# A Fourier filter and a mixer on one core: the prologue's roundings and loads in another order

## The chip, the cores and the metric

The kernel runs on one core of a Trainium2 chip. The metric is the device time of one execution in microseconds; where several are given, the median stands. The engines are TensorE (PE, the matrix unit; its weight loads are shown as PEld), VectorE (DVE), ScalarE (ACT), GpSimd (POOL) and SyncE (SP, which only issues transfers). Each engine executes its own instructions in program order. Transfers (DMA) are issued by SP, ACT and POOL and move data between DRAM and the on-chip memory.

## The reference

Two blocks run one after the other, on 8 batches of 3008 x 256 values. The first filters each column along its 3008 rows in the frequency domain. The second mixes along the rows (token weights, 3008 to 256 to 3008) and then along the columns (channel weights, 256 to 1536 to 256). The sizes below are those of the call.

```python
def _attn_ref(x, filt_r, filt_i):
    X = np.fft.rfft(x, axis=1)
    F = (filt_r + 1j * filt_i)[None, :, :]
    y = np.fft.irfft(X * F, n=x.shape[1], axis=1)
    return y.astype(np.float32)

def _moe_ref(x, w_tok1, w_tok2, w_ch1, w_ch2):
    xt = x.transpose(0, 2, 1)
    h = np.maximum(xt @ w_tok1, 0.0) @ w_tok2
    u = x + h.transpose(0, 2, 1)
    h2 = np.maximum(u @ w_ch1, 0.0) @ w_ch2
    return (u + h2).astype(np.float32)

# x: (8, 3008, 256), filt_*: (1505, 256), float32
# w_tok1: (3008, 256), w_tok2: (256, 3008), w_ch1: (256, 1536), w_ch2: (1536, 256), float64
```

The four weights come in as 8-byte floats and the kernel works in 4-byte floats, so it rounds them on the chip.

## The kernel before, in words

**The filter.** 3008 is 64 times 47. `dft` does a length-64 transform of a batch as 12 matmul steps (`a_unit`, the matmul at L454, one 128 x 512 tile each), and then 32 length-47 steps with the filter's products and the inverse (`b_unit`, matmul L514 and product L522 or L527 to L530; `bi_unit`, matmul L539). Batches go in groups: batch 0 alone, then (1, 2), (3, 4), (5, 6) and 7. `dft` is a generator; each `next` on it emits one step, so that its caller places the steps beside other work. For batch 0 the length-64 results stay on the chip. For the later ones, a step's result is copied by ACT (L460) and stored to `z_tmp`, from where it comes back turned. The inputs `x` of these steps have two buffers: the load for step u + 2 is issued on SP when step u has been emitted. The results of the inverse length-47 steps are stored to `g_tmp` by ACT's queue (L550), two steps to a store, and are read back turned, as six tiles `t4`, by SP (`t4_load`, L587). A row of `t4` is ready when the step that belongs to it has been stored: row r belongs to step r // 4.

**The mixer.** For each batch, `token_sums` (48 matmuls at L593) multiplies the first token weights `w1` with `t4`, ACT takes the maximum with zero (L605), and `u_unit` (for batch 0) multiplies with the second token weights `w2` and adds the filter's last transform (L615, L623). Then 36 *items* follow per batch, six column blocks `m` of six *channel pairs* `jp`. An item runs `up_first` (4 products, L716), the sums `up_middle`, a first part of the preceding pair's `down` (L750), `up_last` (3 products, L732), and the second part of `down`. The weights of the channel mixing are in `chan`, seven combinations to a pair, of which POOL makes some by sums (`combine`, L354 to L358). `mix` is also a generator: it yields after each part of an item (its *place*: 0, 1 or 2), and the main loop decides at each place whether the filter's generator of the next group takes one step there. While the length-64 steps of the first later group last, each place takes one; after that 35 steps are spread over 48 of the places 1 and 2.

**The rounding of the weights.** The weights are cut into 40 tiles, in this order: 12 of `w1`, 16 of `w2` (8 of 64 row groups each, 377 values wide, the last of each half 376), 2 of `w_ch1`, and the ten tiles named `LAST`. A tile passes four phases, each of which is one `next` on the tile's generator: *begin* (the loads; SP issues those of `w1`, POOL all the others), *copy* (one ACT copy of the high words, L260), *middle* (two DVE instructions, L262 and L263) and *end* (two DVE instructions, L266 and L268, and then the two halves are added). For the tiles of `w1` and the first four of `w2` the adding is done by two matmuls in PE (`on_chip`, L301 and L302, into one of the four banks `po`), which `sum_up` emits later, with an ACT copy behind them. For the other tiles DVE adds (L290). `convert_middle` does one middle phase and `sum_up`; `convert_end` does one end phase, one copy phase (two tiles ahead of the end phase), and lets `fill` begin further tiles, up to five beyond those ended (four for `LAST`). `convert` is both. A tile's loads go into a staging buffer that an earlier tile has to leave first. POOL makes the sums of `combine` at the end of a tile that completes a pair.

**The order around the change.** The whole program is emitted in one order by hand (`manual_schedule`). It is: the length-64 steps of batch 0; its length-47 steps `k`, with 20 of the 40 tiles spread beside them in half phases (`IN_B`), and within them the loads of rows 0 to 63 of `t4` (at k = 19 to 24) and of rows 64 to 111 (at k = 30 and 31); the loads of rows 112 to 127; `token_sums` of batch 0; the remaining eight `w1` and `w2` tiles; two more tiles around `u_unit`; then the items, of which the first five carry two tiles of `LAST` each, one ahead of `up_first` and one ahead of `up_last`.

Of the kernel before, what the change touches and what calls it, by code (L numbers as in the profile page):

```python
# [19 lines left out]
N1 = 47  # L20
N2 = 64
NF = N // 2 + 1
D = 256
P = 128
K2 = 32
A = 24
# [15 lines left out]
CW = 32  # L42
CB = P // CW
MT = 6
NG = 8
PARTS = (0, 64, 112)
BY_PE = 4
IN_B = 20
EARLY = 12
GROUPS = ((0,), (1, 2), (3, 4), (5, 6), (7,))  # L50

# [74 lines left out]
def kernel(  # L126
# [116 lines left out]

    early = [(up, "u")] * 2 + [(tp, "t")] * 2 + [(vp, "v")] * 2
    late = [(t2p, "t2"), (t3p, "t3")]
    stages = [(t4p, "t4")] * (A // 2) + early * 3 + late * 5

    def stage(n):
        where, tag = stages.pop(0)
# [76 lines left out]

    def w2_load(i):

        t, g = divmod(i, N2 // NG)
        n = NG * N1  # L330

        more = g + 1 < N2 // NG
        st = stage(512)
        nc.gpsimd.dma_start(st[:, 0:n + more], moe_w_tok2[ts(t, P), ds(g * n, n + more)])
        yield
        dst = w2[:, t].rearrange("p (a h n2) -> p h n2 a", h=2, n2=HALF)[:, :, ds(g * NG, NG), :]

        def some(h, nh, w):
            return (lambda v: bass.AP(tensor=v.tensor, offset=v.offset + h * A, ap=[v.ap[0], [A, nh], [N1, NG], [1, w]]),
                    dst[:, h:h + nh, :, 0:w])  # L340

        parts = [some(0, 2, A)] if more else [some(0, 1, A), some(1, 1, A - 1)]
        if i < BY_PE:
            h = halves(st, n + more, spare_pair())
            yield next(h)
            yield next(h)
            on_chip(ident, *next(h), n + more, parts)
        else:
            yield from rounded(st, n + more, parts, False)
# [23 lines left out]
    def wc2_load(i):  # L373
# [5 lines left out]
        def tile_of(dh):  # L379
# [7 lines left out]
    LAST = ((wc2_load, 0), (wc1_load, 1), (wc1_load, 4), (wc2_load, 1), (wc1_load, 2), (wc2_load, 2), (wc1_load, 5),  # L387
            (wc2_load, 3), (wc2_load, 4), (wc2_load, 5))

    tiles = ([w1_load(i) for i in range(A // 2)] + [w2_load(i) for i in range(TC * N2 // NG)]  # L390
             + [wc1_load(c * (DC // 512), False) for c in range(DH)] + [f(i) for f, i in LAST])
    begin, copy, middle, end = (iter(tiles) for _ in range(4))

    def advance(it):
        s = next(it, None)
        if s:
            next(s, None)
# [5 lines left out]
    def convert():  # L403

        convert_middle()
        convert_end()
# [5 lines left out]
    def convert_end():  # L412
        ended[0] += 1
        advance(end)
        advance(copy)
        fill(5)

    begun = [0]

    def fill(ahead):  # L420
        while begun[0] < len(tiles) and begun[0] < ended[0] + (4 if begun[0] >= len(tiles) - len(LAST) else ahead):
            start()
# [299 lines left out]
    def up_middle(hh, w, g, s):  # L722
        hw = w // 2
        u2 = hh[:, 2, 0:hw]
        v(u2, g[0][:, 1, 0:hw], s[:, 0])
        v(s[:, 1:3], g[1][:, :, 0:hw], u2.unsqueeze(1).to_broadcast([P, 2, hw]))
# [95 lines left out]
    def mix(next_ready):  # L822

        wait = []
        pos, hhs, tts = {}, {}, {}

        def loads(b):
            if b + 1 < B and next_ready(b):
                for c in wait:
                    t4_load(b + 1, c)  # L830
                wait.clear()


        own = ({(3, 2): 0, (4, 2): 1}, {(2, 2): 0, (3, 0): 1, (3, 2): 2, (4, 0): 3})
        new = {(JP - 3, 2): 0, (JP - 2, 0): 1, (JP - 2, 2): 2, (JP - 1, 0): 3}

        def u_parts(b, m, jp, place):
            parts = own[b > 0] if m + 1 < MT else new if b + 1 < B else {}
            part = parts.get((jp, place))
            if part is None:  # L840
                return
            b, m = (b, m + 1) if m + 1 < MT else (b + 1, 0)
            u_part(b, m, part)
            if part == len(parts) - 1:
                if m:
                    wait.append(m)
                todo_v.extend(v_steps(b, m))
                if b and (b, m) < (B - 1, MT - 2):
                    w2m_load((m + 2) % MT)

        to_dram = [f for m in range(MT) for f in w2_sums(m)]
        items = [(b, m, jp) for b in range(B) for m in range(MT) for jp in range(JP)]
        n = MT * JP
        for i in range(len(items) + 1):
            now, old = i < len(items), i >= 1
            convert()
            if now:
                b, m, jp = items[i]
                if i % n == 0:
                    wait.append(0)  # L860
                w = width(m)
                hhs[i] = hp.tile([P, 4, 256], FP32, tag="hh", name="hh")
                g = [bank("pg").rearrange("p (s n) -> p s n", s=2) for _ in range(2)]
                s = up_first(jp, uts[b, m], vts[b, m], w, g)
                up_middle(hhs[i], w, g, s)
            one_step()
            if old:
                bo, mo, jo = items[i - 1]
                tts[i - 1] = tp.tile([P, 4, 256], FP32, tag="t", name="t")
                for f in h_sums(hhs[i - 1], tts[i - 1], width(mo)):  # L870
                    f()
                down(mo, jo, 0, hhs[i - 1], tts[i - 1], pos.setdefault((bo, mo), []))
            if now:
                u_parts(b, m, jp, 0)
            yield b, i % n, 0
            convert()
            if now:
                up_last(jp, uts[b, m], vts[b, m], w, g, s, hhs[i])
            one_step()
            loads(b)  # L880
            yield b, i % n, 1
            if old:
                down(mo, jo, 1, hhs.pop(i - 1), tts.pop(i - 1), pos[bo, mo])
                if jo == JP - 1:
                    todo_v.extend(finish(bo, mo, uts[bo, mo], pos[bo, mo]))
                    one_step()
                    one_step()
            if now:
                if b + 1 < B and i % n == n - 4:
                    h1s[b + 1] = token_relu(b + 1, token_sums(b + 1))  # L890
                u_parts(b, m, jp, 2)
                if jp == JP - 1:
                    while todo_v and m + 1 == MT:
                        one_step()
                if i >= 8 and to_dram:
                    to_dram.pop(0)()
                if i in (28, 29):
                    w2m_load(i - 28)
            loads(b)
            yield b, i % n, 2  # L900
        while todo_v:
            one_step()

    with tc.manual_schedule():
# [6 lines left out]
        for i, _ in enumerate(dft(GROUPS[0])):  # L911
            if i == 0:
                nc.scalar.dma_start(wai_t, wait_d)
            k = i - NXC - 2

            if i < NXC:
                if i in (1, 3, 5, 7, 9):
                    start()
                if i == NXC - 1:
                    advance(copy)  # L920
                    advance(copy)
                    for t, src in ((wa, wa_d), (wai, wai_d), (ident, ident_d)):
                        nc.scalar.dma_start(t, src)
            elif k >= 0:
                while half < 2 * IN_B * (k + 1) // K2:
                    if half % 2:
                        convert_end()
                    else:
                        convert_middle()
                    half += 1  # L930

                if 19 <= k < 25:
                    t4_load(0, k - 19, 0, PARTS[1])
                elif k in (30, 31):
                    for c in range(3):
                        t4_load(0, 3 * (k - 30) + c, PARTS[1], PARTS[2])
        for c in range(A // TC4):
            t4_load(0, c, PARTS[2], P)
        sum_up()
        both = wcp.tile([P, 2, JP, 7, P], FP32, tag="wc", name="wc")  # L940

        chan.extend((both[:, 0], both[:, 1]))
        next(second)
        acc = token_sums(0)
        for _ in range(A // 2 + TC * N2 // NG - IN_B):
            convert()
        h1s[0] = token_relu(0, acc)
        for dh in range(DH):
            convert()
# [13 lines left out]
        for b, i, place in mix(next_ready):  # L963
            if group + 1 < len(GROUPS) and b == GROUPS[group + 1][0]:
                if not done:
                    raise AssertionError("the filter's steps don't fit beside the mixer's")
                group += 1
                done = group + 1 == len(GROUPS)
                todo = iter(()) if done else dft(GROUPS[group + 1]) if group else second
            due = place == 1  # L970
            if group == 0:
                due = spread
                if not spread and place:
                    at += 1
                    due = at * left // places > (at - 1) * left // places or at > places
            if due and not done:
                spread = next(todo, "end")
                done = spread == "end"
# [30 lines left out]
```

## Time and profile before

| What | us |
|---|---|
| median of 4 runs | 2578.13 (2577.76 to 2578.82) |
| profiled execution, its own time | 2583.04 |
| span of the profiled execution | 2581.3 |
| PE busy | 2484.5 (96%) |
| DVE busy | 1922.9 (74%) |
| ACT busy | 677.4 (26%) |
| POOL busy | 582.2 (23%) |
| mean granted clock of PE | 0.990 |

The span is the time from the first to the last instruction of the profiled execution. Times within it are counted from its start. A group's line names the line of the kernel, the engine, and the tiles as out<-in. `ps_` tiles are PE's result banks, `t` of L593 is `t4`, `w` is `w1` or `w2`, `wc` is `chan`, `st` a staging buffer. "SPq" and "ACTq" are the queues' own instructions, which issue transfers. An idle time is followed by what ended it, as far as the profile shows it.

### The profile page before, as it was taken

To read this page: it belongs to the slowest core of one execution; us is meant where nothing else is said; L and a number is where in the kernel's file an instruction comes from. 1 tells how busy PE (TensorE), PEld (TensorE's weight loads), DVE (VectorE), ACT (ScalarE), POOL (GpSimd) and SP (SyncE) were. 2 spreads that over 40 slices of the span, in tenths; PEclk is the share of its full clock that TensorE was granted. 3 is DMA by queue.
4 is the path that set the end of the run, shared out by engine and by line. 5 is a ranking of instruction groups with operands and counts; after the bars stand their busy time and mean duration, and the time that the engine had idled before them with its cause. 6 is when DMAs were issued, how large, how long until landed. Compare 5 with 4: busy or idle time off the path is not lost.

```text
span 2581.3 us, 32269 instructions
## 1 busy us (share of the span) xinstructions
PE 2484.5 (96%) x11196; PEld 2048.4 (79%) x11196; DVE 1922.9 (74%) x3606; ACT 677.4 (26%) x1342; POOL 582.2 (23%) x1057
## 2 busy tenths in 40 slices
PE   7689999999999999999999999999999999999998
PEld 3357666788888777898888777898888888898887
DVE  7857887567686998756676899856788587757776
ACT  5523222122221222212321222212222122212222
POOL 5543322211211112112121111121121121211222
PEclk9889999999999999999999999999999999999999
DMA  9954444333342332213332333213333222111100
GB/s 228 231 145 162 126 131 121 126 97 101 105 128 71 97 107 79 92 48 105 123 106 89 89 112 102 85 37 106 99 95 108 63 79 71 40 31 37 44 13 20
DMA packets 166912, 248.38 MB, mean 96 GB/s; under 512 B 35236, under 2 KB 112410, under 8 KB 166750
## 3 DMA queue, kind: packets, MB, share of 16 engines
q1 hardware_dynamic: 93966, 152.01, 19.5%
q0 software_dynamic: 32832, 46.70, 7.4%
q10 hardware_dynamic: 39952, 47.61, 5.8%
q8 instruction: 89, 1.46, 0.2%
q14 instruction: 73, 0.60, 0.1%
HBM read 168.96 MB, written 77.22 MB: 95 GB/s over the span
## 4 chain that ended last, share of the span: by engine, by line
PE 75%; DVE 16%; DMA 4%; issue 2%; ACT 2%; ACTq 0%; POOL 0%; DVEq 0%; SPq 0%; POOLq 0%
PE ps_po L750 25%; PE ps_pg L716 15%; PE ps_pg L732 11%; PE ps_b L593 4%; DVE t L694 3%; DVE hh L694 3%; PE ps_acc L637 2%; PE ps_b L637 2%; PE ps_acc L593 2%; DVE u L694 2%; DVE s L694 2%; PE ps_acc L615 2%; PE ps_b L615 2%; PE ps_b L514 1%; PE ps_b L539 1%
## 5 line engine op out<-in xcount | busy, mean ns | idle before, releaser
L795 POOL DMA_DIRECT2D out_dram<-r x757 | 410.3, 550 | 1783.2 <-ACT hh L737 759.2
L694 DVE TENSOR_TENSOR hh<-ps_pg,s 128x512 f32<-128x512 f32 (+3 forms) x864 | 483.0, 587 | 348.4 <-ACT s L719 340.7
L737 ACT ACTIVATE hh<-hh 128x512 f32<-128x512 f32 (+1 forms) x576 | 348.1, 621 | 1184.2 <-DVE hh L694 1184.2
L750 PE MATMUL ps_po<-t,wc 128*128 128x256 f32 (+1 forms) x2304 | 535.7, 375 | 6.4 <-DVE t L694 5.4
L750 PEld LDWEIGHTS ps_po<-t,wc 128*128 128x128 f32 x2304 | 434.2, 190 | 131.5 <-issue 52.7
L716 PE MATMUL ps_pg<-v,wc 128*128 128x256 f32 (+1 forms) x1728 | 413.0, 375 | 2.4 <-DVE v L694 2.4
L750 PE MATMUL ps_po<-hh,wc 128*128 128x256 f32 (+1 forms) x1728 | 412.7, 375 | 2.7 <-POOL wc L358 2.5
L716 PEld LDWEIGHTS ps_pg<-v,wc 128*128 128x128 f32 x1728 | 327.5, 190 | 42.0 <-DVE v L694 5.1
L750 PEld LDWEIGHTS ps_po<-hh,wc 128*128 128x128 f32 x1728 | 327.9, 190 | 40.7 <-POOL wc L358 2.9
L732 PE MATMUL ps_pg<-u,wc 128*128 128x256 f32 (+1 forms) x1152 | 294.8, 379 | 3.2 <-DVE hh L694 3.2
L694 DVE TENSOR_TENSOR t<-t,hh 128x256 f32<-128x256 f32 (+1 forms) x576 | 245.9, 427 | 19.9
L732 PEld LDWEIGHTS ps_pg<-u,wc 128*128 128x128 f32 x1152 | 217.4, 191 | 39.7 <-DVE hh L694 12.9
L694 DVE TENSOR_TENSOR s<-ps_pg,hh 128x512 f32<-128x512 f32 (+1 forms) x288 | 196.1, 681 | 30.3 <-PE ps_pg L716 0.5
L694 DVE TENSOR_TENSOR t<-hh 128x512 f32<-128x512 f32 (+1 forms) x288 | 192.8, 669 | 0.6 <-ACT hh L737 0.6
L719 ACT COPY s<-ps_pg 128x256 f32<-128x256 f32 (+1 forms) x288 | 105.8, 367 | 311.8 <-PE ps_pg L716 307.9
L716 PE MATMUL ps_pg<-u,wc 128*128 128x256 f32 (+1 forms) x576 | 168.8, 375 | 0.8 <-DVE hh L694 0.8
L732 PE MATMUL ps_pg<-v,wc 128*128 128x256 f32 (+1 forms) x576 | 169.1, 375 | 0.0
L716 PEld LDWEIGHTS ps_pg<-u,wc 128*128 128x128 f32 x576 | 109.1, 190 | 25.1 <-issue 11.5
L593 PE MATMUL ps_b<-t,w 128*128 128x256 f32 x480 | 106.8, 385 | 23.0 <-issue 22.0
L593 PEld LDWEIGHTS ps_b<-t,w 128*128 128x128 f32 x480 | 92.5, 193 | 36.9 <-issue 22.4
L732 PEld LDWEIGHTS ps_pg<-v,wc 128*128 128x128 f32 x576 | 109.1, 190 | 13.2
L694 DVE TENSOR_TENSOR u<-ps_acc,u 128x512 f32<-128x512 f32 (+3 forms) x105 | 61.1, 582 | 76.8 <-PE ps_acc L637 60.3
(125 smaller groups left out, 2477.4 us busy)
## 6 DMA issues: line engine op xcount, KB each, us to landing
w<-w_tmp SPq DMA_DIRECT2D x35, 896.0 KB
g_tmp<-t ACTq DMA_DIRECT2D x128, 192.0 KB
out_dram<-r POOLq DMA_DIRECT2D x698, 32.0 KB, 1.8
x<-in_x_dram SPq DMA_DIRECT2D x173, 128.0 KB
z_tmp<-t ACTq DMA_DIRECT2D x84, 256.0 KB
t<-z_tmp SPq DMA_DIRECT2D x112, 192.0 KB
t<-g_tmp SPq DMA_DIRECT2D x42, 512.0 KB
wb<-wbi_t SPq DMA_DIRECT2D x80, 224.0 KB
```

The costliest lines, as they stand in the source:

```text
L514: nc.tensor.matmul(ps, wbs[k // WC][0:P if first else KR, k % WC, 0:P], t2, start=True, stop=True)
L539: nc.tensor.matmul(ps[0:KR], wi, p, start=(i == 0), stop=(i == len(parts) - 1))
L593: nc.tensor.matmul(acc[:, t, :], w1[:, a, ts(t, P)], t4[b, a // TC4][:, a % TC4, :], start=(a == 0 and t == 0), stop=(a == A - 1 and t == ...
L615: nc.tensor.matmul(ps[:, ds(q * P, n)], t4[b, c][:, r, ts(dh, P)], wai[:, 0:n], start=(first and q == 0), stop=(not first and q == 3))
L637: nc.tensor.matmul(ps[:, ds(j * hw, hw)], h1[:, n, :], w2m[m % 2][:, at, 0:hw], start=(i < 2 and j == 0), stop=(j == len(todo) - 1))
L694: nc.vector.tensor_tensor(out=out, in0=in0, in1=in1, op=op)
L716: nc.tensor.matmul(ps[:, 0:hw], chan[0][:, jp, n, :], mov, start=True, stop=True)
L719: nc.scalar.copy(out=s[:, 0], in_=g[0][:, 0, 0:hw])
L732: nc.tensor.matmul(ps[:, 0:hw], chan[0][:, jp, n, :], mov, start=True, stop=True)
L737: nc.scalar.activation(out=hs, in_=hs, func=AF.Relu)
L750: nc.tensor.matmul(po[i][:, j, 0:hw], chan[1][:, jp, n, :], mov, start=(jp == 0 and first == 1), stop=(jp == JP - 1 and last == 1))
L795: q.dma_start(rows[g, e, :, ds(h * A + 4 * m, n)], blocks[ts(g, CW), h, e, 0:n])
```

## The change

The tiles of `w2` take ten row groups instead of eight, so there are 14 instead of 16 (the last of each half has four groups). Eight of them instead of four are added by PE. Beside the length-47 steps of batch 0 run 16 tiles instead of 20. The rows of `t4` are loaded in four parts (to 64, 96, 112, 128) instead of three, the new one at k = 26 to 28. Four more tiles are emitted ahead of `token_sums`, and six after it. For the ten tiles of `LAST` the copy phase runs one tile ahead of the end phase instead of two. In the items, the halves of a rounding stand apart: the middle after `up_middle`, the end after the first part of `down`, the next middle ahead of `up_last` and its end after it. `mix` yields at a fourth place, 3, after `up_middle`; the length-64 steps of the first later group are taken at all four places, its further steps at places 1 and 2 as before.

```diff
-NG = 8
-PARTS = (0, 64, 112)
-BY_PE = 4
-IN_B = 20
+NG = 10
+W2G = -(-N2 // NG)
+PARTS = (0, 64, 96, 112)
+BY_PE = 8
+IN_B = 16
...
-    stages = [(t4p, "t4")] * (A // 2) + early * 3 + late * 5
+    stages = [(t4p, "t4")] * (A // 2) + (early * 3)[0:TC * W2G + DH] + late * 5
...
     def w2_load(i):
-        t, g = divmod(i, N2 // NG)
-        n = NG * N1
-        more = g + 1 < N2 // NG
+        t, g = divmod(i, W2G)
+        nn = min(NG, N2 - g * NG)
+        n = nn * N1
+        more = g + 1 < W2G
...
     def convert_end():
         ended[0] += 1
         advance(end)
-        advance(copy)
+        copies()
         fill(5)
+
+    copied = [0]
+
+    def copies():
+        while copied[0] < len(tiles) and copied[0] <= ended[0] + (copied[0] < len(tiles) - len(LAST)):
+            advance(copy)
+            copied[0] += 1
...
+        def late_half(f):
+            if ended[0] < len(tiles):
+                f()
...
         for i in range(len(items) + 1):
             now, old = i < len(items), i >= 1
-            convert()
             if now:
...
                 up_middle(hhs[i], w, g, s)
+                late_half(convert_middle)
+                yield b, i % n, 3
             one_step()
...
             if now:
                 u_parts(b, m, jp, 0)
+            late_half(convert_end)
             yield b, i % n, 0
-            convert()
+            late_half(convert_middle)
             if now:
                 up_last(jp, uts[b, m], vts[b, m], w, g, s, hhs[i])
+            late_half(convert_end)
             one_step()
...
                 if i == NXC - 1:
-                    advance(copy)
-                    advance(copy)
+                    copies()
...
                 if 19 <= k < 25:
                     t4_load(0, k - 19, 0, PARTS[1])
+                elif 26 <= k < 29:
+                    for c in range(2):
+                        t4_load(0, 2 * (k - 26) + c, PARTS[1], PARTS[2])
                 elif k in (30, 31):
                     for c in range(3):
-                        t4_load(0, 3 * (k - 30) + c, PARTS[1], PARTS[2])
+                        t4_load(0, 3 * (k - 30) + c, PARTS[2], PARTS[3])
         for c in range(A // TC4):
-            t4_load(0, c, PARTS[2], P)
-        sum_up()
+            t4_load(0, c, PARTS[3], P)
...
-        acc = token_sums(0)
-        for _ in range(A // 2 + TC * N2 // NG - IN_B):
+        for i in range(IN_B, A // 2 + TC * W2G):
             convert()
+            if i == A // 2 + BY_PE - 1:
+                sum_up()
+                acc = token_sums(0)
         h1s[0] = token_relu(0, acc)
...
             if group == 0:
                 due = spread
-                if not spread and place:
+                if not spread and place in (1, 2):
```

More of the change, by code (lines that the diff above doesn't have):

```diff
@@ L327, in w2_load @@
     def w2_load(i):
-        t, g = divmod(i, N2 // NG)
-        n = NG * N1
-        more = g + 1 < N2 // NG
+        t, g = divmod(i, W2G)
+        nn = min(NG, N2 - g * NG)
+        n = nn * N1
+        more = g + 1 < W2G
         st = stage(512)
-        nc.gpsimd.dma_start(st[:, 0:n + more], moe_w_tok2[ts(t, P), ds(g * n, n + more)])
+        nc.gpsimd.dma_start(st[:, 0:n + more], moe_w_tok2[ts(t, P), ds(g * NG * N1, n + more)])
         yield
-        dst = w2[:, t].rearrange("p (a h n2) -> p h n2 a", h=2, n2=HALF)[:, :, ds(g * NG, NG), :]
+        dst = w2[:, t].rearrange("p (a h n2) -> p h n2 a", h=2, n2=HALF)[:, :, ds(g * NG, nn), :]
         def some(h, nh, w):
-            return (lambda v: bass.AP(tensor=v.tensor, offset=v.offset + h * A, ap=[v.ap[0], [A, nh], [N1, NG], [1, w]]),
+            return (lambda v: bass.AP(tensor=v.tensor, offset=v.offset + h * A, ap=[v.ap[0], [A, nh], [N1, nn], [1, w]]),
                     dst[:, h:h + nh, :, 0:w])
@@ L388 @@
             (wc2_load, 3), (wc2_load, 4), (wc2_load, 5))
-    tiles = ([w1_load(i) for i in range(A // 2)] + [w2_load(i) for i in range(TC * N2 // NG)]
+    tiles = ([w1_load(i) for i in range(A // 2)] + [w2_load(i) for i in range(TC * W2G)]
              + [wc1_load(c * (DC // 512), False) for c in range(DH)] + [f(i) for f, i in LAST])
```

## The prediction

> **What bounds the kernel now.** I read first the forty slices, to see where TensorE (PE) is not full.
>
> ```profile
> PE   7689999999999999999999999999999999999998
> DVE  7857887567686998756676899856788587757776
> DMA  9954444333342332213332333213333222111100
> ```
>
> One slice is 64.5 us. From the fourth on PE is at 9, so what follows the prologue is paid in PE work that the change leaves as it is. Gains and losses can only come from the first three or four slices. Next, busy time by stretch. The columns are length, then busy us of PE, PE weight load, DVE, ACT and POOL, then granted clock, DMA share and GB/s.
>
> ```profile
> 97.50:107.50 10.00, 7.79 (x27) 5.21 (x28) 8.60 (x18) 7.34 (x15) 5.48 (x10) 0.83 0.67 194
> 107.50:117.50 10.00, 1.60 (x7) 0.66 (x5) 9.59 (x22) 2.82 (x6) 1.98 (x4) 0.76 0.99 217
> 117.50:125.00 7.50, 0.00 (x0) 0.00 (x0) 6.99 (x16) 1.64 (x3) 3.37 (x7) 0.50 1.04 239
> 125.00:132.30 7.30, 0.02 (x1) 0.05 (x1) 6.94 (x15) 1.21 (x2) 4.17 (x8) 0.50 0.87 143
> 132.30:155.40 23.10, 23.08 (x96) 19.64 (x96) 3.96 (x8) 0.66 (x1) 1.47 (x3) 0.91 0.42 89
> 163.20:174.20 11.00, 7.78 (x22) 4.07 (x20) 9.67 (x18) 3.38 (x7) 8.43 (x16) 0.84 0.77 239
> 174.20:185.03 10.83, 9.02 (x35) 6.12 (x33) 9.46 (x18) 3.73 (x8) 7.52 (x13) 1.00 0.71 222
> 185.03:198.49 13.46, 10.92 (x35) 7.34 (x36) 10.64 (x21) 5.52 (x12) 7.66 (x12) 0.87 0.75 229
> 198.49:212.10 13.61, 12.00 (x48) 8.01 (x47) 12.21 (x21) 5.54 (x11) 11.41 (x19) 1.00 0.50 161
> ```
>
> Two holes. PE does nothing from 110 to 132.3 and then runs the token sums (L593) for 23.1 us, while DVE has only 4 us of work. Then come the first four channel pairs ("items" 0 to 3; an item runs from one first L716 matmul to the next, here from 163.2, 174.2, 185.0 and 198.5 to 212.1), in which PE idles 3.2 + 1.8 + 2.5 + 1.6 = 9.2 us and DVE is busy 42.0 of 48.9 us. What ends the first hole is in the timeline and in the DMA queue's own waits:
>
> ```profile
> 110.75 0.31 ACTq L550 DMA_DIRECT2D g_tmp<-t  x1
> 125.39 3.13 SPq L587 DMA_DIRECT2D t<-g_tmp  x6
> 132.28 1.19 PE L593 MATMUL ps_b<-t,w 128*128 128x256 f32 x2 [21.96 <-issue]
> SPq L587 <- DMA g_tmp<-t: 34.8, 3, 19.7
> ```
>
> The chain of waits names a channel-weight load and a rounding before 132.28, but the token sums use neither. They use `t4`, whose last rows SP cannot ask for before the last store to `g_tmp` has landed. The store took 14.6 us (110.75 to 125.39), the last six loads and their wait another 6.9. The waits of the four items, PE's, then ACT's and DVE's:
>
> ```profile
> PE ps_acc L454 <- DMA x<-in_x_dram: 2.9, 2, 2.0
> PE ps_po L750 <- POOL wc L358: 2.5, 1, 2.5
> ACT top L260 <- DVE wc L290: 14.7, 5, 5.6
> ACT top L260 <- DMA z_tmp<-t: 9.6, 3, 3.7
> DVE hh L694 <- ACT s L719: 5.4, 4, 2.4
> ```
>
> ACT stands in front of the L260 copy of a later tile until DVE has finished an earlier one, and the copy `s` that DVE needs for the pair's first sums is queued behind it.
>
> **The change, part by part. Rows in four parts.** Before, rows 64 to 111 (6 x 192 KB = 1.18 MB) are read at 107.4, just ahead of the last store. Now rows 64 to 95 (6 x 128 KB = 0.79 MB) go at steps 26 to 28 and only 6 x 64 KB stay there. Steps 26 to 28 lie about 96 to 102 us; in 97.5 to 107.5 the DMA share is 0.67, so there is room. SP waits there for stores it would have waited for anyway, and what is queued behind it are only the next t4 parts, since the last table load goes out at 85.4. SP issues six DMAs more, 0.34 to 0.69 us each in the timeline: 3 us, in place of a 19.7 us wait. The 0.79 MB no longer ahead of the last store are 3.6 us at the 217 GB/s of 107.5 to 117.5. Bounds on what the landing of 14.6 us loses: nothing, if POOL's weight loads hold it up; 10.7 us, if it lands like the store issued at 103.46, which SP saw landed at 107.38, after 3.9 us. I take 4, the bytes' price.
>
> A rule of the Trainium skill speaks against this part: "DMA: Bandwidth & Descriptors", section "Rules for kernel authors", asks to join many small transfers, and its section on the anatomy of one DMA gives each about 2 us of fixed cost. By that, six more in series would be an estimated 12 us lost and the change slower. No run here shows them in series: the twelve loads at 107.38 and after go out half a microsecond apart, so the sum uses that.
>
> **16 tiles, 14 token tiles.** Beside the 33 steps 16 roundings run instead of 20, and the loads begun by their end are 21 instead of 25. Nine token tiles of 471 x 8 bytes x 128 = 482 KB stand against thirteen of 386 KB: 4.3 against 5.0 MB, 0.7 MB less, 2.6 us at the 261 GB/s of 40 to 60 us. The steps are 2.5 us each (76 us for 31) with DMA at 0.9 to 1.05, so I take 2 us earlier; bounds 0 (the filter loads set the pace) and 5 (DVE, 4 half roundings of 1.1 us saved in the last steps, sets it as well). DVE per token tile, from rows of 377 (0.34, 0.55, 0.35, 0.55, add 0.81) and 512 columns (0.42, 0.69, 0.42, 0.69): about 2.1 without the add, 3.1 with it. Four through PE come ahead of the token sums: 4 x 2.1 = 8.4 us from about 108, so 117, nine before they are due; their matmuls, 1.7 us a tile, fall in PE's hole, and their copies on ACT, which has 1.6 of 7.5 us busy there. Behind them 6 x 3.1 and two channel tiles of 2.9 make 24.4 us more on DVE, until 141, under the token sums (126 to 149). If that cover went, each us past 149 would cost one. The 23.1 us of the token sums stay, slow start included (clock 0.50 before, 0.91 in it).
>
> So the token sums start 4 + 2 = 6 us earlier, near 126.3, and all behind them too.
>
> **Roundings in halves, steps after each quarter pair.** The same 10 tiles are rounded in items 0 to 4; DVE's sum is unchanged, its order isn't: the pair's first sums come ahead, ACT's copy runs one tile ahead instead of two, so `s` no longer stands behind it (5.4 us of DVE waits, to nothing at best). Against that POOL: `combine` starts later in the item, by the sums now ahead of it (1.1 + 1.7 us), and the chain of ten sums, four DMA issues and five sums that ran 177.0 to 189.9 already held PE 2.5 us at L358. By the rows laid end to end PE waits there some 4 us longer, while DVE goes on with the next rounding. I take the two as even. What remains is the fourth length-64 step (L454) per item: the 22 left fit in 5.5 items instead of 7.3. Each is 0.86 us of PE work brought into PE's idle time of items 0 to 3: 4 x 0.86 = 3.4 us, less 0.4 for ACT's copies of it (0.58 each, one more in the same queue): 3 us. Bounds: 8 faster, if most of the 9.2 us fill up; 8 slower, by x (next part). The length-47 steps of the next batches then lie two items earlier, at the same density (35 over 48 places, four whole cycles of the six pairs), so I cost their move at nothing, give or take 2.
>
> Sum: 2581.3 - 6 - 3 = 2572.3 us of span. The profiled execution took 2583.04, 1.7 more than its span and 4.9 more than the median 2578.13 of the runs; so 2569 on the scale of the runs.
>
> **The rivals.** *The store lands no sooner* (chance 0.20): POOL's tiles, now longer rows, hold the rings, as 217 to 239 GB/s up to 125 would allow. Only some 1 to 2 us of the start and 3 of the items are left: 2574. For it: the share is 1.04 after 117.5, when SP's reads are nearly through. Against: the 3.9 us of the store with little around it.
>
> *Slower: x cannot be fed* (0.14). There are two buffers for x, so step u+2 waits for a load issued after step u. From the first issue to the step: 162.44 to 167.05 = 4.6 us, 168.85 to 173.27 = 4.4, 172.38 to 178.39 = 6.0, 236.18 to 240.21 = 4.0, and PE waited each time. With landing L, two steps need L + 1.1 us; 22 steps 11 (L + 1.1). To that 1.8 items without them (6.2 us each, as item 8 at 6.0) add 11.3. Before, this stretch took 81.8 us (163.2 to the end of the last step at 245.0). L = 4.6 gives 62.7 + 11.3 = 74, no loss. L = 6.0 gives 89.4: 7.6 slower, and with the 6 of the start 1.6 net. From L = 6.3 the net is over 5.2 us and it decides; at 6.5 it is 7.1 slower: 2585. Against: only one of four was that long, amid the heaviest weight loads.
>
> *Both terms near their far ends* (0.16): the start 12 us earlier, items 6: 2560.
>
> **How the numbers follow.** My forecast, both terms at my values, has 0.50: 2569. About 0.2% (5.2 us) is what a measurement can tell from no change. Faster by more: forecast and far ends, 0.66; within: 0.20; slower: 0.14. The range goes from the far end, 2559, to the x rival at L = 6.1, 2581; left out are most of the 0.14 and a tail below.
>
> **What would show it.** Right: the last store lands within 11 us; token sums start at 124 to 128; PE idle in items 0 to 3 below 6 us; ACT's wait for L290 nearly gone; the L454 steps over by item 5. Wrong: SP's last loads still over 13 us behind the last store; PE waits on x over 6 us in items 0 to 5; PE at L750 waiting on POOL over 7 us; DVE still at tail tiles when the token sums end.

## The result, and the profile after

The changed kernel takes 2582.5 us (median of 34 runs, 2576.1 to 2590.8) against 2578.2 (52 runs, 2573.6 to 2585.9): a ratio of 1.0015, 95% interval 1.0009 to 1.0021, so about 4 us slower. A second set, with 11 runs of it, gave 1.0005 (0.9993 to 1.0016), which leaves no change possible. Nine microseconds faster was forecast, with 2559 to 2581 as the range. The time is outside it, on the other side.

The profiled execution says the opposite: 2577.1 us of span against 2581.3. It took 2578.9, 3.6 below the median of its kernel; the one of before was 4.9 above its own. So two profiled executions can't be subtracted here, and each stage needs more than one of each. First what the changed one shows. The forty slices:

```profile
PE   7879999999999999999999999999999999999998
DVE  7667888576686998756676899856788587757776
DMA  9964444233332332213332233213333222111100
```

PE's first dip is shallower (the second slice went from 6 to 8). The slice behind it, in which the items begin, fell from 8 to 7; the rest of PE's row is as it was. By stretch (length, busy us of PE, weight load, DVE, ACT and POOL, then clock, DMA share, GB/s):

```profile
107.50:117.50 10.00, 8.31 (x26) 3.80 (x24) 7.69 (x16) 6.43 (x12) 1.65 (x3) 1.00 0.78 240
117.50:123.10 5.60, 3.67 (x12) 1.80 (x12) 4.54 (x11) 3.13 (x7) 1.50 (x3) 1.00 0.97 238
123.10:144.00 20.90, 20.85 (x97) 18.02 (x95) 19.32 (x38) 4.48 (x8) 9.49 (x19) 1.00 0.78 185
151.76:164.97 13.21, 8.86 (x24) 4.83 (x23) 8.56 (x17) 5.07 (x9) 5.29 (x10) 0.87 0.72 225
164.97:178.41 13.44, 9.95 (x38) 6.67 (x37) 9.91 (x18) 4.89 (x9) 6.72 (x13) 1.00 0.72 221
178.41:194.30 15.89, 11.12 (x38) 6.94 (x36) 9.65 (x19) 4.89 (x9) 8.29 (x15) 0.90 0.78 243
194.30:208.82 14.52, 14.17 (x49) 9.74 (x48) 9.88 (x18) 5.66 (x10) 6.28 (x11) 0.87 0.50 171
```

The token sums are the third line: from 123.1 to 144.0, beside 19.3 us of DVE work, where before they ran from 132.3 to 155.4 beside 4.0. The last four lines are items 0 to 3. They take 57.1 us, where they took 48.9; PE idles 13.0 in them instead of 9.2, and in item 3 its matmuls themselves are slower (14.2 us busy, clock 0.87). The timeline of the last store, the last rows of `t4` and the token sums, from ACT's queue, SP's queue and PE:

```profile
113.52 0.31 ACTq L560 DMA_DIRECT2D g_tmp<-t  x1
117.59 2.62 SPq L597 DMA_DIRECT2D t<-g_tmp  x6
123.07 0.38 PE L603 MATMUL ps_b<-t,w 128*128 128x256 f32 x1
```

The store lands in 4.1 us instead of 14.6. Now the waits of items 0 to 3 (total us, times, longest), PE's, DVE's and ACT's:

```profile
PE ps_b L464 <- DMA x<-in_x_dram: 10.4, 6, 3.7
PE ps_acc L464 <- DMA x<-in_x_dram: 1.5, 1, 1.5
PE ps_po L760 <- POOL wc L360: 0.7, 1, 0.7
DVE hh L704 <- ACT s L729: 10.9, 4, 6.6
ACT t L470 <- PE ps_b L464: 20.3, 7, 6.2
ACT top L261 <- DVE wc L291: 0.5, 1, 0.5
```

PE waits 11.9 us for x (3.9 before). ACT no longer stands before its copies (14.7 us became 0.5), but stands 20.3 us (0.7 before) behind the length-64 step that PE is held at, and `s` with it: DVE waits 10.9 us for `s`, where the prediction had hoped for nothing.

### The profile page after: what moved, and what is told of

Same layout as the page of the kernel before. It is cut to its first block, busy times and chain, and to the rows that moved or that the text cites. A ratio compares the mean times of both kernels' runs of the same rounds, so it can differ in the third digit from the quotient of the medians.

```text
span 2577.1 us, 32295 instructions
## 1 busy us (share of the span) xinstructions
PE 2492.3 (97%) x11212; PEld 2049.7 (80%) x11212; DVE 1914.3 (74%) x3591; ACT 680.2 (26%) x1345; POOL 576.4 (22%) x1055
## 4 chain that ended last, share of the span: by engine, by line
PE 73%; DVE 16%; DMA 5%; issue 2%; ACT 2%; POOL 0%; SPq 0%; ACTq 0%; DVEq 0%; POOLq 0%
PE ps_po L760 25%; PE ps_pg L726 15%; PE ps_pg L742 10%; DVE t L704 4%; PE ps_acc L603 3%; PE ps_b L603 3%; DVE hh L704 3%; PE ps_b L647 2%; PE ps_acc L647 2%; DVE u L704 2%; DVE s L704 2%; PE ps_b L625 2%; PE ps_acc L625 2%; DMA x<-in_x_dram 1%; PE ps_b L464 1%
## 5 line engine op out<-in xcount | busy, mean ns | idle before, releaser
L704 DVE TENSOR_TENSOR u<-ps_b,u 128x512 f32<-128x512 f32 (+3 forms) x105 | 61.1, 582 | 76.8 <-PE ps_b L647 60.3
L704 DVE TENSOR_TENSOR u<-ps_acc,u 128x256 f32<-128x256 f32 (+3 forms) x105 | 59.5, 566 | 61.3 <-PE ps_acc L647 42.4
L603 PE MATMUL ps_acc<-t,w 128*128 128x256 f32 x384 | 83.7, 380 | 1.1 <-ACT t L555 1.1
```

Source lines behind the costliest of these rows:

```text
L603: nc.tensor.matmul(acc[:, t, :], w1[:, a, ts(t, P)], t4[b, a // TC4][:, a % TC4, :], start=(a == 0 and t == 0), stop=(a == A - 1 and t == ...
L704: nc.vector.tensor_tensor(out=out, in0=in0, in1=in1, op=op)
```

## The experiments

All ratios are to runs of the kernel before on the same chip. Its medians there were 2577.6 to 2579.6 us, so rows of different chips are compared by their ratios; after_again, prologue, steps3 and steps4 share one chip, after_nox, steps3_nox, parts4 and tiles16 a second, after_x4, p4_steps4_x4, p4_halves and before_again a third. "Start" is when item 0 begins in the profiled execution, "items" the time from the start of item 0 to that of item 32, by which all steps of batches 1 and 2 are done. What follows item 32 differs by 2.4 us at most between the profiles.

| kernel | median us (runs) | ratio, 95% interval | start | items |
|---|---|---|---|---|
| before, first profile | 2578.2 (52) | 1 | 163.2 | 324.6 |
| before_again | 2577.1 (1) | | 156.4 | 325.5 |
| changed, first profile | 2582.5 (34) | 1.0015 (1.0009 to 1.0021) | 151.8 | 331.2 |
| after_again | 2579.0 (11) | 1.0005 (0.9993 to 1.0016) | 149.6 | 329.2 |
| parts4 | 2572.1 (8) | 0.9977 (0.9966 to 0.9989) | 153.3 | 323.9 |
| tiles16 | 2579.5 (11) | 1.0006 (0.9997 to 1.0015) | 161.6 | 324.2 |
| prologue | 2573.0 (11) | 0.9976 (0.9965 to 0.9986) | 153.9 | 325.3 |
| steps4 | 2586.3 (12) | 1.0025 (1.0015 to 1.0035) | 154.5 | 334.1 |
| steps3 | 2577.0 (12) | 0.9994 (0.9983 to 1.0004) | 155.4 | 326.5 |
| steps3_nox | 2575.8 (12) | 0.9991 (0.9981 to 1.0002) | 156.1 | 328.1 |
| after_nox | 2567.5 (5) | 0.9963 (0.9950 to 0.9976) | 151.7 | 320.9 |
| after_x4 | 2568.2 (6) | 0.9956 (0.9940 to 0.9972) | 149.2 | 321.7 |
| p4_steps4_x4 | 2569.5 (12) | 0.9966 (0.9956 to 0.9976) | 149.8 | 321.0 |
| p4_halves | 2576.8 (12) | 0.9988 (0.9976 to 1.0001) | 155.1 | 325.8 |
| p4_lead1 | 2574.6 (11) | 0.9981 (0.9972 to 0.9990) | 153.2 | 326.6 |
| p4_lead1_steps4_x4 | 2571.1 (6) | 0.9972 (0.9956 to 0.9988) | 151.6 | 324.4 |
| p4_nosums | 2567.9 (5) | 0.9959 (0.9945 to 0.9972) | 152.9 | 321.2 |
| p4_halves_nosums | 2571.4 (5) | 0.9968 (0.9955 to 0.9980) | 151.3 | 324.8 |
| p4_nosums_x4 | 2569.3 (5) | 0.9960 (0.9946 to 0.9975) | 150.1 | 320.7 |
| p4_halves_nosums_x4 | 2563.6 (5) | 0.9936 (0.9923 to 0.9949) | 152.6 | 316.5 |

**Which half of the change costs.** The theory after the result: the prologue's part gains, and the fourth length-64 step per item outruns the loads of x. Its first rival: the order of the halved roundings makes the items longer. Its second: the early start is luck of one execution.

after_again is the changed kernel, unaltered.

> The changed kernel once more, for a second profiled execution of it beside timed runs. In its first one the token sums start 9.2 us earlier than before (123.1 against 132.3), the items 11.4 us earlier, and PE waits 11.9 us for x in items 0 to 3 (3.9 before). Feed theory (the fourth length-64 step per item outruns the loads of x): token sums again before 127, waits for x again over 8 us, time about 2582. Sample theory (the early start is luck of that execution): token sums at 128 or later in this one, waits for x whatever they are, time about 2582.

The token sums start at 120.8 and PE waits 11.0 us for x in items 0 to 5: both again. The start is no luck. (Both profiled executions of the changed kernel lie below the medians of their runs, by 3.6 and 4.3 us. What a median execution loses beyond the stages shown is in no profile.)

steps3:

```diff
-                due = spread
+                due = spread and place != 3
```

> The changed kernel with the length-64 steps of the first later group at three places of an item (0, 1, 2) instead of four; the roundings stay in halves. Feed theory: PE waits for x under 5 us in items 0 to 3, 6 to 9 us faster than the changed kernel, so 2573 to 2577. Order theory (the halves of the roundings, POOL's sums and ACT's copies behind them, make the items longer, not x): items 0 to 3 stay near 57 us, time 2580 to 2584.

2577.0, at the slow end of what the feed theory allowed; items 0 to 3 take 48.2 us, not the 57 of the order theory, and the items shrink to 326.5. Taking the fourth place out gives back about 2 us by these medians, 3 to 5 by the items, not the whole loss. PE's waits in its items 0 to 3:

```profile
PE ps_acc L464 <- DMA x<-in_x_dram: 7.5, 4, 3.0
PE ps_po L760 <- POOL wc L360: 2.2, 1, 2.2
```

Even at three places the waits for x are well over the 3.9 us of before, and over the 5 that were expected.

prologue is the changed kernel with `convert()` at the heads again, the copy two tiles ahead and no fourth place:

```diff
-        while copied[0] < len(tiles) and copied[0] <= ended[0] + (copied[0] < len(tiles) - len(LAST)):
+        while copied[0] < len(tiles) and copied[0] <= ended[0] + 1:
...
+            convert()
             if now:
...
-                late_half(convert_middle)
-                yield b, i % n, 3
...
-            late_half(convert_end)
             yield b, i % n, 0
-            late_half(convert_middle)
+            convert()
...
-            late_half(convert_end)
```

> Only the prologue's part of the change (14 token tiles, 8 of them through PE, 16 tiles beside the length-47 steps, rows in four parts, token sums after four more tiles); the items as in the kernel before, with whole roundings and three places. Feed theory: items 0 to 3 again near 49 us, the earlier start is kept: 2567 to 2571. Order theory: the same. Sample theory: the start moves by 3 us or less in the median: 2575 to 2578.

2573.0, 2 us over the expected range: the earlier start is kept, and items 0 to 3 take 49.5 us as expected. Faster than both kernels. On the same chip the changed kernel took 2579.0, so the change's part in the items costs 6.0 us where a gain of 3 was forecast.

steps4 is the kernel before with the fourth place only:

```diff
                 up_middle(hhs[i], w, g, s)
+                yield b, i % n, 3
...
-                if not spread and place:
+                if not spread and place in (1, 2):
```

> The kernel before with the fourth place alone: a length-64 step after the pair's first sums as well; the prologue and the roundings as before. Feed theory: PE waits for x over 7 us in items 0 to 3, 2 to 8 us slower than before: 2580 to 2586. Order theory and the forecast: 3 us faster by the steps moved into PE's idle time: 2575.

2586.3, 8 us slower, at the far side of the feed theory. The place that was forecast to gain 3 us costs 8 by itself. PE's waits in its items 0 to 3:

```profile
PE ps_acc L454 <- DMA x<-in_x_dram: 7.2, 4, 2.1
PE ps_acc L454 <- issue: 3.6, 2, 2.9
PE ps_b L454 <- DMA x<-in_x_dram: 2.1, 3, 0.9
```

That is 9.3 us for x, and 3.6 at the same matmul that the profile puts down to nothing.

**Is it the feeding?** A step must not wait, so its load was taken away: 22 of the 24 steps read again the tiles that the first two steps read.

```diff
+            old_x = xs[u]
             a_unit(*u)
             if i + ahead < len(todo):
-                x_load(*todo[i + ahead])
+                if bs == GROUPS[1]:
+                    xs[todo[i + ahead]] = old_x
+                else:
+                    x_load(*todo[i + ahead])
```

> The changed kernel without the loads of x for 22 of the 24 length-64 steps of batches 1 and 2: these steps read the two tiles that were loaded first, so no step waits for x and 5.8 MB are not moved (the filter of these two batches is left out in that sense). Feed theory: PE's waits for x in items 0 to 5 go from 11 to 12.6 us to nothing, items 0 to 31 shrink from 329 to 331 us to 318 to 322, time 2570 to 2574, and it is as fast as or up to 3 us faster than the same with three places. Order theory: what is lost lies in the order of roundings, sums and copies; it stays 2 us or more slower than the same with three places, near 2577.

> The changed kernel with length-64 steps at three places, and without the same loads of x. Feed theory: it waited 7.5 us for x in items 0 to 5 with them, so 3 to 6 us faster than 2577: 2571 to 2574. Order theory: 2575 to 2577, x being hidden behind the roundings anyway.

With four places the loads are worth 11 to 15 us (2567.5 against 2579.0 and 2582.5), with three 1 us (2575.8 against 2577.0), which is within the noise. Fed, the fourth place is 8 us better than three, more than the 3 at most that were expected; hungry, 2 to 5 us worse. The expectation for three places missed: the wait for x goes there, but another takes its place. PE's waits of steps3_nox in items 0 to 3:

```profile
PE ps_po L764 <- POOL wc L360: 7.8, 1, 7.8
PE ps_pg L730 <- DVE hh L708: 1.5, 2, 0.8
```

That is the wait for POOL's sums, which the prediction priced at 4 us more than 2.5 and then called even. It had stood behind the waits for x. (This profile is the slowest of its kernel's 12 runs.) The kernel with four places and without the loads has the same wait, and no other:

```profile
PE ps_po L764 <- POOL wc L360: 7.4, 1, 7.4
```

So without the loads some 7.5 us remain at either number of places, and what differs is what x had cost above that. PE's idle time in items 0 to 3 is 9.7 us with the loads and 9.6 without at three places, 13.0 and 7.4 at four.

Buffers or traffic? The seventh `t4` buffer stands idle in the first batch's items, so two of its halves can hold x, and all the work is done:

```diff
-        t = where.tile([P, xc, dc], FP32, tag=tag, name="x")
+        slot = len(x_seen) % 4
+        if b in GROUPS[1]:
+            x_seen.append((b, c))
+        if b in GROUPS[1] and slot >= 2:
+            if not x_more:
+                x_more.append(t4p.tile([P, TC4, D], FP32, tag="t4", name="x_more"))
+            t = x_more[0][:, 2 * (slot - 2):2 * (slot - 1), :]
+        else:
+            t = where.tile([P, xc, dc], FP32, tag=tag, name="x")
...
-        ahead = NXC if first else XB
+        ahead = NXC if first else 4 if bs == GROUPS[1] else XB
```

> The changed kernel with four buffers for x instead of two while batches 1 and 2 are transformed (the two more are halves of the seventh t4 buffer, which stands idle in the first batch's items); all work is done. Feed theory: PE's waits for x in items 0 to 5 fall from 11 to 12.6 us to under 3 and the time comes near that without the loads, 2568 to 2573. Traffic theory (it was the 5.8 MB of loads beside the weights' loads, not the two buffers, that cost): 2577 to 2581, little better than the changed kernel.

2568.2, as fast as without the loads, with the same bytes moved. PE's waits in its items 0 to 3:

```profile
PE ps_po L769 <- POOL wc L360: 4.2, 1, 4.2
PE ps_acc L473 <- ACT t L479: 1.7, 1, 1.7
PE ps_b L473 <- ACT t L479: 1.5, 2, 1.1
```

No wait for x is left, though all of it is loaded. It was the buffers, so the distance between issue and use, and not the traffic.

**The prologue's terms.** parts4 is the kernel before with the `PARTS` and `t4_load` lines of the diff alone; tiles16 is the prologue's part without them.

> The kernel before with the rows in four parts alone. The prediction's term is 4 us (the last store lands sooner): 2574. Rival (the new tiles give the start, the reads are hidden anyway): 2577 to 2579.

> The prologue's part of the change with the rows in three parts as before: 14 token tiles, 8 through PE, 16 beside the length-47 steps. The prediction's term is 2 us: 2576. Rival (this part carries the 5 us that the whole prologue's part gained): 2572 to 2574, and then the four parts alone give nothing.

The four parts carry all of it: 5.5 us. The tiles alone give nothing (1.0006, 0.9997 to 1.0015).

> The kernel before once more, for a second profiled execution. From its median 2578, and 2047 us from item 36 on and 371 from item 0 to 36 in the first one, item 0 starts near 158 us in a usual execution, 5 us earlier than the 163.2 of the first, because the last store landed late in that one. Expected here: item 0 at 155 to 161, token sums at 124 to 130. If it is at 162 or later again, the four parts gain by another way.

Item 0 at 156.4: as expected, nearly 7 us ahead of the first profile. Its last store took 8.5 us to land (113.4 to 121.9).

**The fourth place with whole roundings.** p4_steps4_x4 joins parts4, the edit of steps4 and that of after_x4.

> The kernel before with two things alone: the rows in four parts, and the fourth place with four buffers for x. Roundings whole, at the heads, tiles as before. Feed theory: the fourth place, fed, is worth the 3 us that the prediction gave it, on top of the 5.5 of the four parts: 2567 to 2570. Order theory (the halves are what makes a fourth place pay; with whole roundings ahead of the pair the copies of ACT stand in line): 2573 to 2578.

2569.5 against 2572.1 of the parts alone (0.9966 against 0.9977, on two chips, and the intervals overlap). That agrees with the 3 us that the prediction gave the fourth place, but does not show them: four buffers with whole roundings and three places were run only without POOL's sums (below), where they gained nothing. At least the place no longer costs 8 us, and it needs no halves for that.

**The halves.** p4_halves joins the four parts and the halves' lines, p4_lead1 the four parts and `copies()` with its lead of one alone.

> The kernel before with two things alone: the rows in four parts, and the roundings in halves with ACT's copy one tile ahead; three places, two buffers for x. Order theory (the sums of POOL start later in the item and PE waits for them): 2 to 5 us slower than the four parts alone, 2574 to 2577. The prediction's even account: 2571 to 2573.

> The four parts, and ACT's copy of a tile of LAST one tile ahead instead of two; roundings whole and at the heads. Copy theory (the lead of one costs): 2575 or more. POOL theory and order theory: 2570 to 2573, as the four parts alone or a little faster by the 20.6 us that ACT no longer stands before its copies.

p4_halves: 4.7 us slower than the parts alone by the medians, 2.8 by the ratios, on two chips and with intervals that overlap. The clearer pair is steps3 and prologue, on one chip, which differ only in the halves and in ACT's copy, one tile ahead instead of two: 2577.0 against 2573.0, 4.0 us. (There the fourth place alone costs 8 us, the halves 4 and both together 6.0, so the two do not add.) p4_lead1: 2574.6, between the theories, 2.5 slower by the medians, 1.0 by the ratios, with intervals that overlap. PE waits 8.1 us for x in it (5.1 in parts4); DVE's wait moved from `s` to the copy itself:

```profile
DVE top L262 <- ACT top L260: 9.2, 4, 5.2
```

p4_nosums and p4_halves_nosums leave out POOL's sums of the ten last tiles; DVE writes zeros in their place:

```diff
             for jp in range(2 * q, 2 * q + 2):
-                combine(chan[0][:, jp:jp + 1])
+                if q == 0:
+                    combine(chan[0][:, jp:jp + 1])
...
-        combine(chan[1][:, i:i + 1])
...
+        for part in (chan[0][:, 2:JP], chan[1]):
+            nc.vector.memset(part[:, :, 2:4, :], 0.0)
+            nc.vector.memset(part[:, :, 5, :], 0.0)
```

> The four parts without POOL's sums of the ten last tiles (the combinations of the channel weights are set to zero instead, 3 to 4 us of DVE in its idle time), whole roundings. PE waited 1.9 us for POOL in it, and DVE's instructions beside POOL's take 0.67 to 0.83 us instead of 0.42 to 0.69. All theories: 2568 to 2572.

> The same without POOL's sums, roundings in halves. POOL theory: the cost of the halves is gone, within 1.5 us of p4_nosums or faster. Order theory: still 3 to 5 us slower than p4_nosums.

3.5 us of difference remain by the medians, 2.3 by the ratios, with intervals that overlap; so POOL alone is hardly it. PE's waits of p4_halves_nosums in items 0 to 3 show what stepped in, 10.0 us for x where p4_nosums waits 4.3:

```profile
PE ps_acc L462 <- DMA x<-in_x_dram: 8.9, 3, 4.8
PE ps_b L462 <- DMA x<-in_x_dram: 1.1, 1, 1.1
```

Then both kernels with four buffers for x.

> The four parts, whole roundings, without POOL's late sums, with four buffers for x and three places. All theories: its wait for x of 4.3 us goes, part of it hidden: 2564 to 2568.

> The same with roundings in halves. Two-waits theory: within 1.5 us of p4_nosums_x4, or faster. Order theory (DVE waits for ACT's copy s, 14.3 us without POOL's sums): 3 us or more slower than it, 2568 to 2571.

2563.6 against 2569.3: with neither wait, halves are 5.6 us *faster* than whole roundings. (p4_nosums_x4 is no faster than p4_nosums, against expectation; its profile was the fastest of its five runs.) So the order on DVE is good, and with two buffers the halves cost by the wait for x, even without POOL's sums. That the wait for POOL costs as much once x is fed is argued from the 7.8 us of steps3_nox, not shown. The nearest pair with four buffers and all sums is after_x4 and p4_steps4_x4, on one chip, which differ in the tiles too: 2568.2 with halves, 2569.5 without, so no cost, though PE waits 4.2 us for POOL in the first. POOL may there eat what the order gains.

> The four parts, the copy rule, and the fourth place with four buffers for x; whole roundings, tiles as before. If the copy rule gains 1 us and the fed fourth place 3, 2567 to 2569; if the copy rule costs, 2571 or more.

2571.1: no better than p4_steps4_x4 without the copy rule.

## Why the prediction was wrong

**The start: right in size, by terms that offset each other.** 6 us were forecast, 4 from the store's landing and 2 from the steps. By the timed runs the prologue's part gives 5.0 us and the four parts alone 5.5. With twenty tiles, the three profiles with rows in three parts (before, before_again, steps4) can be set against the nine with four (parts4 and all p4). The last store lands after 14.6, 8.5 and 7.8 us, against 2.5 to 4.8: 6.9 less in the mean, over the byte price of 4. From the first of the last loads to the token sums it is 2.5 us less in the mean. But the store itself goes out 3.6 us later (110.8, 113.4 and 111.1, against 113.5 to 119.2), so the reads at steps 26 to 28, which the prediction took as free, may delay the last steps. Together the token sums start 5.8 us earlier, so that the sum came near is in part luck.

The 2 us of the sixteen tiles failed. With rows in three parts their last store is issued at 115.9 (tiles16), no earlier than with twenty; with four at 110.9 to 117.2, 1.4 earlier in the mean, which the next paragraph takes back. The prediction's rule of the Trainium skill, "DMA: Bandwidth & Descriptors", section "Rules for kernel authors", to join small transfers, would have made this part a loss; the four parts gained 5.5 us with six transfers more. The 2 us of fixed cost that it set beside the rule stand in that page's section on the anatomy of one DMA for transfers that GpSimd issues; these reads are issued by SP.

**The token sums' duration, and the tiles ahead of them.** It was held at 23.1 us. It is 20.9 in the changed kernel (23.08 to 20.85 us of PE, clock 0.91 to 1.00), where the matmuls of the tiles through PE run up to the token sums. In tiles16 they end 4.3 us ahead of them, and the token sums take 23.0 us at a clock of 0.91. The gain is lost again just ahead: the token sums stand behind these tiles in PE's order, and PE waits for DVE's rounding of the last one.

```profile
122.18 1.06 PE L303 MATMUL ps_po<-both,ident 128*128 128x471 f32 x2 [0.76 <-DVE both L269]
```

The prediction had these tiles done on DVE at 117, nine before they were due. In the seven profiles with sixteen tiles and four parts the token sums start at 123.7 in the mean, in the nine with twenty tiles at 121.3; the items start at 152.5 and 152.2. So a later start and a shorter run cancel, and the tiles give nothing.

**The base.** The sum was made against one execution whose last store had landed 14.6 us after its issue. From the medians the usual start of item 0 is near 158 us, not 163.2; it was 163.2, 156.4 and 154.5 in the three profiles with the unchanged prologue. That does not shift the terms much, but it hid that the stage scatters by several microseconds between executions.

**The step that failed: the length-64 steps brought into PE's idle time.** "4 x 0.86 = 3.4 us, less 0.4": 3 us of gain were taken for the items. The part of the change that lies in the items costs 6.0 us instead (2579.0 against 2573.0 on one chip), and the fourth place by itself 8. The work did move, and the steps were over by item 5 as predicted. But the 22 steps took 75.3 and 73.4 us, and with 1.8 items without them (the prediction's 11.3) that is 84.7 to 86.6 against 81.8 before: 2.9 to 4.8 slower instead of 3 faster. The items as a whole grew by 4 to 7 us. PE idled 13.0 us in items 0 to 3, where below 6 was the sign of being right. PE's idle time was counted as free, when over a third of it already was waiting for the same loads: 3.9 us of 9.2. A step put there needs its x one place sooner, and with two buffers the load's issue can't move with it. With four buffers the same schedule takes 2568.2 us.

**The rival was the right one, with too high a point of decision.** "x cannot be fed" had a chance of 0.14, a mechanism, and a decision at landings of 6.3 us. Where PE waited, issue to step was 4.2 to 7.5 us in the changed kernel, 5.3 in the mean of eight. By the rival's formula 11 (5.3 + 1.1) = 70 us, no loss; 73 to 75 were measured. (Its decision point was also a little off by its own sum: at 6.3 it gives 4.9 us net, and 5.2 at 6.33.) The formula spreads waits evenly; in one row of in-order engines a late x also holds `up_last`, ACT's copies and `s`, and in the changed kernel's first profile PE's clock was 0.87 to 0.90 in three of the first four items (in its second it was 0.88 in one; in the kernel before it was 0.84 and 0.87 in two, so the clock does not tell the kernels apart). The sign for it ("waits on x over 6 us in items 0 to 5") was there: 12.6.

**The halves: "even" was wrong as made, right as an order.** ACT's wait before its copies went as predicted. POOL's wait was 7.8 us once x was out of the way (predicted 2.5 + 4). With two buffers for x the halves cost 4.0 us (steps3 against prologue). The ledger had taken the saved wait for `s` as the balance, but `s` stood behind the next thing.

## What to carry to other kernels

Idle time of an engine is room for more work only if that work's inputs arrive sooner too: before a step is moved up, look at what the step now waits for, and count buffers against issue-to-landing times. The same schedule lost 1 to 4 us with two buffers and gained 10 with four (2568.2, the lowest median of a complete version here); and when one wait is taken away, price the one that stands behind it. Where executions scatter by as much as the effect, take several profiles of the stage that scatters, since one may start from its unlucky end.

## What was not expected of the hardware

The landing of the last 192 KB store varied from 2.5 to 14.6 us: 7.8 to 14.6 in the four profiles where six 192 KB reads were issued just ahead of it, 2.5 to 5.1 in the sixteen where these were 64 KB each. 256 KB loads of x took 4.2 to 7.5 us from issue to step where PE waited for them, in items 0 to 5 of one execution.
